# One written order for a random-feature attention and mixer kernel, with the first four quads transposed on TensorE, joined tail angles and later low-rank loads

## The chip, the cores and the metric

The kernel runs on one core of a Trainium2 chip. The metric is device time in microseconds (us), where lower is better. "PE" is TensorE, "DVE" VectorE, "ACT" ScalarE, "POOL" GpSimd and "SP" SyncE.

Ratios are the mean time of one kernel's fast runs over the mean of the other's fast runs in the same rounds, so they are not quite the ratio of the medians that are quoted beside them. Intervals in brackets are 95% intervals of the ratio.

## The reference

Attention with random features, per batch and head, and then a mixer and a two-layer network on the attention's output:

```python
batch, n_heads, seq, head_dim, n_features = 8, 8, 576, 64, 128
def phi(x):
    proj = np.einsum('bhsd,md->bhsm', x, omega)
    return np.concatenate([np.cos(proj), np.sin(proj)], axis=-1) / np.sqrt(m)
q_p, k_p = phi(q), phi(k)
kv = np.einsum('bhsm,bhsd->bhmd', k_p, v);  z = np.sum(k_p, axis=2)
num = np.einsum('bhsm,bhmd->bhsd', q_p, kv);  den = np.einsum('bhsm,bhm->bhs', q_p, z)
attn = num / den                       # den kept away from zero
x = attn.transpose(0, 2, 1, 3).reshape(8, 576, 512)
u = x + (x.transpose(0, 2, 1) @ U @ V).transpose(0, 2, 1)      # U 576x32, V 32x576
out = u + np.maximum(u @ w_ch1, 0.0) @ w_ch2                   # 512 -> 2048 -> 512
```

The network needs 1152 matmuls of 128x128 by 512 columns (576 for each layer). They are most of the work.

## The kernel before

A *group* is two heads of one batch, so there are four groups in a batch and 32 in all. A *quad* is two groups: its keys and queries are loaded by one DMA each, cast to bf16 on the way, transposed so that the head dimension lies on the partitions, and multiplied by `WT` (omega) to give angles. ACT takes their sines, POOL adds a quarter turn, ACT takes the sines again (the cosines). Then come `kv`, `num`, a normalisation `x`, the low-rank mixer (`hu`, `hn`, `hnt`) giving `u`, a DMA transpose of `u`, and the two layers `w1` and `w2`.

Every piece is an operation with a name. A planner decides the order and the PSUM banks from costs:

```python
add(("ak", g), PE, 0.27, ak, needs=kmain + ["WT"], takes=A, rank=(0, g, 0), slack=slack)
...
def order(self):                      # greedy list scheduler
    ...
            at = max([free[o.engine]] + [done[n] + o.slack for n in o.needs ...])
            ...                       # candidate banks: the one that is free first
            key = (at, o.rank)        # earliest start, then rank: attention before MLP on PE
    ...
order = plan.order()
with tc.manual_schedule():
    for o in order:
        o.emit()
```

Quad 0 is transposed on PE, with evictions on DVE and ACT. All others are transposed by DMA. The tail tokens (the ninth of nine token slots) have their own angle eviction `ut` and their own normalisation:

```python
BY_PE = (0,)
def tpd(name=name, n=n):              # quads 1 to 15
    nc.sync.dma_start_transpose(transposed(name, n), held.pop((name, n)).rearrange("p i e -> p (i e)"))
def ak(g=g, n=n):                     # 64-row matmuls
    for j in range(4):
        for e in range(2):
            r, c = at(g, 2 * j + e)
            nc.tensor.matmul(pk[:, e, j * P:(j + 1) * P], kT[r, c, :], WT[r, :])
def kv(fs, g=g, n=n):                 # 64-row matmuls: 18 with a group's sines, 18 with its cosines
    ...
            nc.tensor.matmul(kv_ps[:, hh, o], ft[r, f, 0, c:c + M], vq[n % NV][r, NS * (g % 2) + s, :], ...)
def load_low_rank():                  # on the ACT queue, early
    nc.scalar.dma_start(Vf, moe_V.unsqueeze(0).to_broadcast([4, R, S]))
    ...
```

`ak`, `at`, `aq` and `kv` use 64 of the 128 rows of the PE array, `hu` uses 32 columns of it, and `hnt` 64 columns. `w1`, `w2`, `num` and `hn` use the full array.

## Time and profile before

Three runs gave a median of 406.62 us (405.06 to 406.68). The profiled span is 404.4 us.

| engine | busy us | share of the span |
|---|---|---|
| PE | 358.1 | 89% |
| ACT | 225.7 | 56% |
| DVE | 199.4 | 49% |
| POOL | 123.1 | 30% |

The first view is the page of the kernel before: first its line of engine totals, then the busy share of PE, the granted clock of PE and the busy share of the DMA engines in 40 equal slices of the span (each digit is tenths of a slice, about 10 us wide).

```profile
PE 358.1 (89%) x3416; PEld 176.3 (44%) x3462; DVE 199.4 (49%) x340; ACT 225.7 (56%) x280; POOL 123.1 (30%) x132
...
PE   3266769689679999999999999999999999999995
PEclk9998769879959999999999999999999999999999
DMA  8999999999999787799744141023115121111223
```

PE is short of work in the first twelve slices, and the DMA engines are full in just those. The windows view of the kernel before puts numbers to it. Its columns are: stretch, length, busy time (and count) of PE, weight loads, DVE, ACT and POOL, then the granted clock, the DMA share and GB/s.

```profile
0.00:34.00 34.00, 15.66 (x272) 11.22 (x275) 18.05 (x38) 19.67 (x21) 20.85 (x32) 1.00 1.06 194
34.00:60.00 26.00, 17.73 (x189) 9.64 (x187) 12.33 (x25) 12.55 (x17) 13.11 (x15) 0.74 1.21 178
60.00:90.00 30.00, 24.70 (x267) 11.41 (x270) 17.62 (x29) 19.52 (x24) 13.64 (x15) 0.89 1.22 192
90.00:120.00 30.00, 23.74 (x320) 12.77 (x322) 21.41 (x37) 17.98 (x18) 16.88 (x17) 0.83 1.13 219
120.00:250.00 130.00, 127.78 (x1489) 62.77 (x1507) 91.83 (x154) 99.48 (x119) 51.68 (x49) 1.00 0.66 123
```

PE is busy 81.83 of the first 120 us (the sum of the first four rows), and 98% of the time from 120 to 250 us. The clock is below 1 in three of the four early stretches. A caution: the clock figure of the opening is not to be trusted. It reads 1.00 up to 34 us, but in the timeline sixteen `num` matmuls took 1.04 us at 25.45 and 0.68 us at 28.32. So clocks are compared only after 34 us below.

The table of PE's waits in the kernel before (engine and line, what it waited for, then us in total, times, longest) says for what PE stood:

```profile
PE ps L351 <- DMA kT<-kraw: 11.3, 2, 8.2
...
PE ps L561 <- DMA W2b<-in_moe_w_ch_dram: 2.9, 1, 2.9
PE ps L548 <- DMA uT<-u: 2.5, 1, 2.5
```

L351 is `ak`, which waits for keys transposed by DMA. L561 is `w2`, waiting for the last piece of W2 (used at 81.7 us). L548 is `w1`, waiting for the first transposed `u` (at 114.5 us). All three are DMA transfers.

This is the timeline of PE in the kernel before (start, duration, operation, count of matmuls run together; durations overlap by the depth of the pipeline):

```profile
170.56 1.03 PE L548 MATMUL ps<-uT,W1b 128*128 128x512 bf16 x4
171.51 0.40 PE L351 MATMUL ps<-WT,kT 64*128 64x128 bf16 x8
171.84 1.04 PE L561 MATMUL ps<-W2b,hid 128*128 128x512 bf16 x4
172.81 0.75 PE L394 MATMUL ps<-vq,ft 64*128 64x65 bf16 x36
173.40 0.38 PE L370 MATMUL ps<-qT,WT 64*128 64x512 bf16 x2
173.71 1.04 PE L548 MATMUL ps<-uT,W1b 128*128 128x512 bf16 x4
174.68 0.23 PE L362 MATMUL ps<-WT,kT 64*128 64x128 bf16 x1
```

The part of the array in use stands after the operation: `128*128` is all of it, `64*128` half.

The groups view of the kernel before gives the mean duration of the two layers' matmuls (line, form, count, busy us, mean ns, idle before):

```profile
L561 PE MATMUL ps<-W2b,hid 128*128 128x512 bf16 x537 | 140.1, 383 | 7.1 <-issue 3.4 <-DMA W2b<-in_moe_w_ch_dram 2.9
L548 PE MATMUL ps<-uT,W1b 128*128 128x512 bf16 x512 | 134.5, 389 | 2.8 <-DMA uT<-u 2.5
```

Of the 576 `w2` matmuls 537 are recorded; of all 3462 matmuls 46 are missing from this trace, although their weight loads are in it. The missing ones show as short waits for "issue" (3.4 us), so the idle time of PE in this trace is overstated, and its busy time understated, by at least that much.

### The profile page before, as it was taken

How to read it: one execution, taken by the hardware profiler on the slowest of the kernel's cores; microseconds unless marked ns; L12 is line 12 of the kernel's file. 1: busy time of each engine (PE TensorE's matmuls, PEld its weight loads, DVE VectorE, ACT ScalarE, POOL GpSimd, SP SyncE). 2: the span in 40 equal slices, each digit the busy share in tenths (PEclk: the TensorE clock that was granted, in tenths of full speed). 3: DMA queues.
4: the chain of work that ended last, by engine and by line, in shares of the span. 5: the costliest groups of instructions: out<-in, count | busy, mean ns of one | idle time of the engine just before them, and what ended most of it. 6: DMA issues, size and time to landing. Idle time of an engine off the chain costs nothing.

```text
span 404.4 us, 8121 instructions
## 1 busy us (share of the span) xinstructions
PE 358.1 (89%) x3416; PEld 176.3 (44%) x3462; DVE 199.4 (49%) x340; ACT 225.7 (56%) x280; POOL 123.1 (30%) x132
## 2 busy tenths in 40 slices
PE   3266769689679999999999999999999999999995
PEld 2155334344434444445444544544444444444442
DVE  4367436558847678777676368536313010101021
ACT  3757357564758889787696468737423333333300
POOL 5849065444653365365154023303000000000000
PEclk9998769879959999999999999999999999999999
DMA  8999999999999787799744141023115121111223
GB/s 221 162 189 171 176 196 225 207 155 206 251 192 138 152 123 160 159 192 140 170 118 73 41 92 28 2 54 78 28 39 105 26 48 31 38 43 27 52 54 79
DMA packets 75930, 46.90 MB, mean 116 GB/s; under 512 B 54644, under 2 KB 66804, under 8 KB 75892
## 3 DMA queue, kind: packets, MB, share of 16 engines
q1 hardware_dynamic: 62512, 32.22, 39.9%
q0 software_dynamic: 12672, 13.34, 22.4%
q10 hardware_dynamic: 708, 0.80, 0.6%
q8 instruction: 27, 0.44, 0.5%
q14 instruction: 11, 0.09, 0.1%
HBM read 37.21 MB, written 9.44 MB: 115 GB/s over the span
## 4 chain that ended last, share of the span: by engine, by line
PE 77%; DMA 11%; DVE 4%; issue 3%; POOL 2%; ACT 2%; POOLq 0%
PE ps L548 31%; PE ps L561 29%; PE ps L394 4%; PE ps L408 4%; DMA kT<-kraw 3%; DMA W2b<-in_moe_w_ch_dram 3%; PE ps L351 2%; DMA qraw<-in_q_dram 2%; PE ps L370 2%; POOL ang L384 2%; DMA uT<-u 2%; ACT ft L380 2%; DVE ang L329 1%; PE ps L512 1%; PE ps L413 1%
## 5 line engine op out<-in xcount | busy, mean ns | idle before, releaser
L380 ACT ACTIVATE ft<-ang 128x1024 bf16<-128x1024 int16 (+2 forms) x130 | 144.0, 1142 | 40.1 <-POOL ang L384 24.6
L553 ACT ACTIVATE hid<-ps 128x512 bf16<-128x512 f32 x144 | 85.5, 595 | 112.5 <-PE ps L548 111.9
L561 PE MATMUL ps<-W2b,hid 128*128 128x512 bf16 x537 | 140.1, 383 | 7.1 <-issue 3.4
L548 PE MATMUL ps<-uT,W1b 128*128 128x512 bf16 x512 | 134.5, 389 | 2.8 <-DMA uT<-u 2.5
L329 DVE TENSOR_SCALAR ang<-ps 128x1024 int32<-128x1024 f32 (+2 forms) x97 | 89.4, 943 | 43.3 <-PE ps L351 13.3
L384 POOL TENSOR_SCALAR ang<-ang 128x1280 int32<-128x1280 int32 (+1 forms) x64 | 73.6, 1153 | 97.3 <-ACT ft L380 96.8
L548 PEld LDWEIGHTS <-W1b 128*128 128x128 bf16 x576 | 53.2, 99 | 65.7 <-issue 8.5
L561 PEld LDWEIGHTS <-hid 128*128 128x128 bf16 x576 | 52.4, 98 | 65.2 <-issue 7.7
L573 DVE TENSOR_TENSOR o<-ps,u 128x512 f32<-128x512 f32 x32 | 22.1, 690 | 94.7 <-PE ps L561 91.4
L394 PEld LDWEIGHTS <-ft 64*128 64x128 bf16 x1152 | 23.4, 99 | 18.8 <-issue 12.1
L394 PE MATMUL ps<-vq,ft 64*128 64x65 bf16 x1152 | 28.8, 198 | 1.9 <-ACT ft L380 0.9
L408 PE MATMUL ps<-kvb,ft 128*128 128x65 bf16 x512 | 23.2, 198 | 6.1 <-ACT ft L380 5.1
L408 PEld LDWEIGHTS <-ft 128*128 128x128 bf16 x512 | 20.6, 101 | 13.0 <-ACT ft L380 5.7
L351 PE MATMUL ps<-WT,kT 64*128 64x128 bf16 x256 | 14.4, 240 | 11.9 <-DMA kT<-kraw 11.3
L287 POOL CAST vq<-vraw 128x1152 bf16<-128x1152 f32 x16 | 18.4, 1149 | 20.9 <-PE ps L394 15.8
L514 DVE TENSOR_TENSOR u<-ps,x 128x1024 bf16<-128x1024 f32 x16 | 19.5, 1221 | 6.8 <-PE ps L512 5.5
L425 DVE TENSOR_TENSOR x<-ps,rec 128x512 bf16<-128x512 f32 x32 | 22.1, 692 | 1.1
L280 POOL DMA_DIRECT2D kraw<-in_k_dram x15 | 10.9, 727 | 35.3 <-DMA kT<-kraw 35.2
L398 DVE CAST kvb<-ps 128x260 bf16<-128x260 f32 x32 | 13.6, 424 | 12.2 <-PE ps L394 12.0
L351 PEld LDWEIGHTS <-kT 64*128 64x128 bf16 x256 | 8.4, 103 | 22.4 <-DMA kT<-kraw 12.0
L548 PE MATMUL ps<-utailT,W1b 128*128 128x512 bf16 x64 | 16.4, 379 | 0.1
L370 PE MATMUL ps<-qT,WT 64*128 64x512 bf16 x64 | 13.5, 413 | 2.2 <-DVE ang L329 1.2
(60 smaller groups left out, 140.1 us busy)
## 6 DMA issues: line engine op xcount, KB each, us to landing
vraw<-in_v_dram SPq DMA_DIRECT2D x16, 576.0 KB, 4.8
out_dram<-o SPq DMA_DIRECT2D x72, 128.0 KB, 2.4
kraw<-in_k_dram POOLq DMA_DIRECT2D x15, 288.0 KB, 6.7
qraw<-in_q_dram POOLq DMA_DIRECT2D x15, 288.0 KB, 7.7
W1b<-in_moe_w_ch_dram POOLq DMA_DIRECT2D x4, 512.0 KB, 10.2
W2b<-in_moe_w_ch_dram POOLq DMA_DIRECT2D x4, 512.0 KB, 13.2
ang<-in_k_dram SPq DMA_DIRECT2D x1, 288.0 KB, 3.0
ang<-in_q_dram ACTq DMA_DIRECT2D x1, 288.0 KB, 4.7
```

The source lines that it names most:

```text
L329: nc.vector.tensor_scalar(out=dst, in0=src, scalar1=TO_UNITS, scalar2=None, op0=ALU.mult)
L351: nc.tensor.matmul(pk[:, e, j * P:(j + 1) * P], kT[r, c, :], WT[r, :])
L370: nc.tensor.matmul(pq[:, e, :], WT[r, :], held["qT", n][r, c:c + 4, :])
L380: nc.scalar.activation(out=held["ft", g].rearrange("p f a c -> p f (a c)")[:, f, lo:hi], in_=low[:, lo:hi, 0], func=ACT.Sin, scale=TO_RAD)
L384: nc.gpsimd.tensor_scalar(out=ang, in0=ang, scalar1=TURN / 4.0, scalar2=1.0, op0=ALU.add, op1=ALU.mult)
L394: nc.tensor.matmul(kv_ps[:, hh, o], ft[r, f, 0, c:c + M], vq[n % NV][r, NS * (g % 2) + s, :], start=(s == 0), stop=(s == NS - 1))
L408: nc.tensor.matmul(nd[:, t // 2, 2 * (t % 2) + hh, :], ft[:, f, 1, c:c + P], kvb[:, hh, f, :], start=(f == 0), stop=(f == 1))
L425: nc.vector.tensor_tensor(out=x[:, :, hp * P:(hp + 1) * P].rearrange("p (a t) (h d) -> p a t h d", a=2, h=2), in0=nd[:, :, 0:4, 0:D], in1= ...
L548: nc.tensor.matmul(one(("w1", b, f)), W1b[:, f // 4, ct, f % 4 * P:(f % 4 + 1) * P], uT[:, :, ct, :], start=(ct == 0), stop=(ct == NCT - 1))
L553: nc.scalar.activation(out=held["hid", b][:, f, :], in_=one(("w1", b, f)), func=ACT.Relu)
L561: nc.tensor.matmul(one(("w2", b, t, 0)), held["hid", b][:, f, t * P:(t + 1) * P], W2b[:, f, :], start=(f == 0), stop=(f == NFT - 1))
L573: nc.vector.tensor_tensor(out=o, in0=one(("w2", b, t, 0)), in1=u[:, t, :], op=ALU.add)
```

## The change

The intent is to take DMA work out of the opening, where DMA is full, to have the keys of the first quads earlier, to spare DVE some instructions, and to replace the planner by one order that was written (found elsewhere) for all engines and PSUM banks. The operations lose their costs and ranks, and a list of words `name@bank` is walked:

```diff
+ORDER = """
+begin first/k om ident first/q ld/k/0 ld/q/0 ld/k/1 ld/q/1 cast/k ldv/0 omb tpp/k/0/0@0 omt@5 tp/k/0/0 cast/q gate WT low tpp/k/0/1@6
+tpp/q/0/0@3 tp/k/0/1 tpp/q/0/1@0 tp/q/0/0 ld/k/2 ak/0@6 tp/q/0/1 uk/0 ld/q/2 ak/1@2 at/0@0 W1/0 uk/1 aq/0@5 sk/0 pk/0 uq/0 aq/1@1 sk/1
 ... (63 lines cut)
+"""
-    def order(self):                  (greedy planner, cut)
+    def run(self, order):
+        for word in order.split():
+            text, _, at = word.partition("@")
+            name = names[text]
+            _, emit, needs, takes, frees = self.ops[name]
+            assert name not in issued and all(n in issued for n in needs), word
+            if takes:
+                self.banks[name] = range(int(at), int(at) + takes)
+            ...
+            emit()
-    BY_PE = (0,)
+    BY_PE, BY_SCA = (0, 1, 2, 3), (0,)         # quads 1 to 3: nine transposes into two banks,
+                                                # one 1152-column copy on DVE
-        nc.scalar.dma_start(Vf, moe_V.unsqueeze(0).to_broadcast([4, R, S]))
+        nc.sync.dma_start(Vf, moe_V.unsqueeze(0).to_broadcast([4, R, S]))
+    add("gate", DVE, lambda: nc.vector.memset(low_f[:, S - 1:S + 1], 0.0))
+    add("low", SP, load_low_rank, needs=["gate"])
-            (nc.sync).dma_start(held["v", n], quad(v, n))          (shortened)
+            (nc.sync if n else nc.gpsimd).dma_start(held["v", n], quad(v, n))
@@ uk @@
-                units(held["ang", g][:, 0, 0:1024], ...)           (and ut: a second instruction for 256 columns)
+            for lo, hi in ((0, 512), (512, 1024)) if g == 0 else ((0, 1280),):
+                units(ang[:, lo:hi], src[:, lo:hi])
@@ norm @@
-                held["x", b] = xp.tile([P, NT, C], BF16, name="x")
+                held["x", b] = xp.tile([P, NT + 1, C], BF16, name="x")
-            nc.vector.tensor_tensor(out=x[:, :, ...], ...)         (and a second one for xtail)
+            nc.vector.tensor_tensor(
+                out=x[:, :, hp * P:(hp + 1) * P].rearrange("p t (h d) -> p h t d", h=2),
+                in0=nd[:, :, :, 0:D], in1=rec.unsqueeze(3).to_broadcast([P, 2, NT + 1, D]), op=ALU.mult)
```

Smaller parts that came along: the first keys are loaded from the ACT queue, omega is loaded without its copy, the first queries are cast on ACT, the sine's warm-up moved to the end, and the PSUM layout of `num` changed for the joined normalisation.

## The prediction

> **What bounds the kernel now.** TensorE (PE) is busy 358 of 404 us (engine table), unevenly: by the windows view 98 to 99% from 120 us on, but 82 of the first 120 us, partly at a low granted clock (0.66 in 50 to 60, 0.51 in 110 to 120). Counting matmuls at warm spacing (512 columns 0.215 us: eight take 1.90, four 1.04), I estimate only 59 us of full-clock work in the first 114.5 us: some 56 us lost there, about 20 in the rest.
>
> The DMA engines are the reason: their share is 0.9 to 1.3 in every 10 us up to 120 us, mostly below 1 later. PE's early waits are for DMA: quad 1's transposed keys at 21.8 (8.2 us), a later quad's at 51.7 (3.2), the last W2 piece at 81.7 (2.9), the first transposed u at 114.5 (2.5). The first MLP matmul starts at 41.4. The trace's DMA packets show why: one transposed 288 KB tile is 1152 packets of 256 B at 28 ns, about 2.0 us of all sixteen engines, as much as loading it (256 packets at 128 ns). A quad costs some 6 us to load and 4 more to transpose.
>
> **What the change does.**
> - Quads 1 to 3 are transposed on PE: 54 more 128-column matmuls, estimated 3 us plus pipeline ends, and six 1152-column copies on VectorE (about 0.9 us each, scaled from 0.48 for 640). This takes 12 us of DMA work out of the saturated stage, and the two longest PE waits.
> - Low-rank loads go behind the first quads; the first value load goes behind four key/query loads.
> - Tail angles join the key angles: 31 evictions of 0.41 us go, their columns add about 0.27 each to the larger one; the 0.27 us tail normalisation joins the 0.69 us one. VectorE falls some 10 us, but is half idle: little gain.
> - The written order places loads, banks and engine order anew. A second activation-table load (1.28 us) appears at the start, mostly hidden.
> - Other PE work stays: the floor after the ramp does not move.
>
> **On the critical path.** ScalarE needs about 4.6 us of sines per group (2 x 1.27 + 2 x 1.05). With keys in time, four groups take about 19 us from about 9 us: first MLP matmul estimated at 32 us, not 41.4. W2's last piece should land near 66, not 81.7 (estimated DMA work ahead of it: eight weight pieces at 3.3, five quads loaded, one transposed, 61 us). The first transposed u is used near 95, not 114.5, at equal attention progress. I expect 20 us from the ramp and a few from higher clock. The Trainium skill (TensorE: Matmul & The Clock Gate, "What's actually happening") says an idle window of about 3.4 us halves the clock; this trace agrees roughly: after the 2.88 us wait four matmuls took 1.87 us, elsewhere 1.04.
>
> **Prediction: 384 us, 373 to 396.** Faster by over 2%: 0.91; within: 0.06; slower: 0.03.
>
> **To check.** DMA share near 1 until about 95 us; no PE wait over 3 us for keys of quads 1 to 3; first MLP matmul at 30 to 35 us; PE above 97% busy from about 95 us; VectorE below 192 us; some 6900 fewer 256 B packets.
>
> **What would make it wrong.** A fixed order makes PE wait where a load is later than planned: weights or quad 4's transposes in 40 to 90 us. If weights remain the limit, the gain shrinks to about 10 us. Transposes inside the dense stage would cost a few us.

## The result and the profile after

The changed kernel took 368.5 us in the median of four runs (364.91 to 371.55, one of them slow), beside 406.65 us of the kernel before (405.06 to 407.5). The ratio is 0.9036 [0.8954, 0.9119], faster. The direction was right. The size was not: 368.5 us lies below the range of 373 to 396. A second measurement on another chip, in the last rounds, gave 367.35 us and 0.8998 [0.8956, 0.904]. All outputs are right.

The page of the kernel after, the same lines (its span is 363.1 us, so a slice is 9.1 us):

```profile
PE 346.7 (95%) x3516; PEld 178.8 (49%) x3516; DVE 195.0 (54%) x283; ACT 226.1 (62%) x282; POOL 122.2 (34%) x131
...
PE   4679999999999999999999999999999999999994
PEclk9668999999999999999999999999999999999999
DMA  8999979999989999799955920106100640052033
```

Two things happened, not one. PE's idle time fell from 404.4 - 358.1 = 46.3 us to 363.1 - 346.7 = 16.4 us. And PE's *busy* time fell by 11.4 us, although 54 matmuls were added (3462 weight loads before, 3516 after). That second fall is the one that the prediction ruled out. (The profile after has all its matmul records. With the 3.4 us of missing records moved from idle to busy, the fall in busy time is about 15 us and that in idle time about 26.5.) The windows of the kernel after:

```profile
0.00:34.00 34.00, 22.51 (x376) 17.45 (x377) 25.22 (x47) 24.90 (x26) 27.99 (x39) 0.80 1.03 207
34.00:60.00 26.00, 25.88 (x337) 14.36 (x334) 18.00 (x23) 23.21 (x30) 12.64 (x14) 1.00 1.08 175
60.00:90.00 30.00, 30.00 (x423) 16.02 (x416) 26.43 (x39) 24.03 (x26) 15.25 (x16) 1.00 1.04 179
90.00:120.00 30.00, 30.00 (x412) 15.62 (x409) 24.85 (x37) 27.36 (x32) 19.49 (x21) 1.00 0.93 198
```

PE is busy 108.39 of the first 120 us, at full clock from 34 us on. The DMA share is still about 1 up to 90 us: the engines stay as full, but with other transfers. PE's waits in the kernel after:

```profile
PE ps L310 <- DVE kraw L282: 4.4, 1, 4.4
PE ps L402 <- DVE ang L339: 2.3, 2, 1.4
PE ps L378 <- DVE ang L339: 2.3, 2, 1.4
```

The waits for transposed keys, for W2 and for `u` are gone. The 4.4 us is the start, before the first load has landed (the kernel before waits 4.2 us at the same place for omega). The timeline of PE in the kernel after, in its dense part, shows how the half-array work is bundled:

```profile
198.06 1.89 PE L554 MATMUL ps<-uT,W1b 128*128 128x512 bf16 x8
199.88 0.46 PE L402 MATMUL ps<-vq,ft 64*128 64x65 bf16 x18
200.18 0.38 PE L378 MATMUL ps<-qT,WT 64*128 64x512 bf16 x2
200.40 0.39 PE L362 MATMUL ps<-WT,kT 64*128 64x128 bf16 x8
200.62 0.22 PE L354 MATMUL ps<-WT,kT 64*128 64x128 bf16 x1
...
201.11 2.76 PE L566 MATMUL ps<-W2b,hid 128*128 128x512 bf16 x12
```

Here `kv` (L402), query angles (L378), key angles (L362) and tail angles (L354) stand next to each other, and twelve `w2` matmuls follow. I counted the round trips from full-array to part-array work and back, from the weight loads between 34 and 330 us: 106 before, 55 after. The groups of the two layers in the kernel after:

```profile
L566 PE MATMUL ps<-W2b,hid 128*128 128x512 bf16 x576 | 136.0, 379 | 0.0
L554 PE MATMUL ps<-uT,W1b 128*128 128x512 bf16 x512 | 121.8, 379 | 0.3 <-ACT hid L559 0.2
```

The means are 379 ns where they were 383 and 389: among the recorded matmuls of the two layers, 25 ran at half clock before (634 ns) and none after.

| event | before | predicted | after |
|---|---|---|---|
| first `w1` matmul, us | 41.4 | 32 | 35.5 |
| last piece of W2 landed, us | 81.4 | 66 | 57.6 |
| first `w1` on a transposed `u`, us | 114.5 | 95 | 78.5 |
| PE idle before 120 us (windows) | 38.2 | - | 11.6 |
| PE idle after 120 us (rest of the span) | 8.1 | - | 4.8 |

### The profile page after: what moved, and what is told of

It is laid out like the page before. It is cut to its first block, busy times and chain, and to the rows that moved or that the text cites. A ratio compares the mean times of both kernels' runs of the same rounds, so it can differ in the third digit from the quotient of the medians.

```text
span 363.1 us, 8210 instructions
## 1 busy us (share of the span) xinstructions
PE 346.7 (95%) x3516; PEld 178.8 (49%) x3516; DVE 195.0 (54%) x283; ACT 226.1 (62%) x282; POOL 122.2 (34%) x131
## 4 chain that ended last, share of the span: by engine, by line
PE 91%; DVE 5%; DMA 1%; POOL 1%; issue 1%; ACT 0%; POOLq 0%; DVEq 0%
PE ps L566 35%; PE ps L554 34%; PE ps L402 6%; PE ps L416 5%; DVE ang L339 3%; PE ps L362 2%; PE ps L378 2%; PE ps L519 2%; PE ps L310 1%; DMA kraw<-in_k_dram 1%; PE ps L421 1%; PE ps L527 1%; PE ps L471 1%; PE ps L473 1%; DVE x L432 1%
## 5 line engine op out<-in xcount | busy, mean ns | idle before, releaser
L559 ACT ACTIVATE hid<-ps 128x512 bf16<-128x512 f32 x144 | 84.3, 594 | 88.4 <-PE ps L554 87.7
L566 PE MATMUL ps<-W2b,hid 128*128 128x512 bf16 x576 | 136.0, 379 | 0.0
L554 PE MATMUL ps<-uT,W1b 128*128 128x512 bf16 x512 | 121.8, 379 | 0.3 <-ACT hid L559 0.2
L339 DVE TENSOR_SCALAR ang<-ps 128x1280 int32<-128x1280 f32 (+3 forms) x66 | 85.4, 1315 | 16.1 <-PE ps L378 7.2
L402 PE MATMUL ps<-vq,ft 64*128 64x65 bf16 x1152 | 25.6, 195 | 2.3 <-DVE ang L339 2.3
L402 PEld LDWEIGHTS <-ft 64*128 64x128 bf16 x1152 | 22.8, 97 | 9.1 <-issue 6.3
L432 DVE TENSOR_TENSOR x<-ps,rec 128x640 bf16<-128x640 f32 x32 | 26.4, 825 | 1.1
L416 PE MATMUL ps<-kvb,ft 128*128 128x65 bf16 x512 | 22.1, 197 | 0.8 <-DVE kvb L406 0.8
L378 PE MATMUL ps<-qT,WT 64*128 64x512 bf16 x64 | 13.8, 397 | 2.3 <-DVE ang L339 2.3
L511 DVE CAST hu<-ps 128x512 bf16<-128x512 f32 x7 | 4.8, 690 | 20.1 <-PE ps L473 14.1
L554 PE MATMUL ps<-utailT,W1b 128*128 128x512 bf16 x64 | 14.8, 379 | 0.0
L430 DVE RECIPROCAL ps<-ps 128x10 f32<-128x10 f32 x32 | 7.2, 225 | 12.3 <-PE ps L421 12.1
L362 PE MATMUL ps<-WT,kT 64*128 64x128 bf16 x256 | 13.5, 231 | 0.1
```

Source lines behind the costliest of these rows:

```text
L339: nc.vector.tensor_scalar(out=dst, in0=src, scalar1=TO_UNITS, scalar2=None, op0=ALU.mult)
L378: nc.tensor.matmul(pq[:, e, :], WT[r, :], held["qT", n][r, c:c + 4, :])
L416: nc.tensor.matmul(nd[:, hh, t, :], ft[:, f, 1, c:c + P], kvb[:, hh, f, :], start=(f == 0), stop=(f == 1))
L432: nc.vector.tensor_tensor(out=x[:, :, hp * P:(hp + 1) * P].rearrange("p t (h d) -> p h t d", h=2), in0=nd[:, :, :, 0:D], in1=rec.unsqueeze ...
L554: nc.tensor.matmul(one(("w1", b, f)), W1b[:, f // 4, ct, f % 4 * P:(f % 4 + 1) * P], uT[:, :, ct, :], start=(ct == 0), stop=(ct == NCT - 1))
L559: nc.scalar.activation(out=held["hid", b][:, f, :], in_=one(("w1", b, f)), func=ACT.Relu)
```

## The experiments

The theories at the start were these. The transposes on PE give the gain, because they free DMA in the opening; or the written order gives it, whatever does the transposes. Rivals for parts of it are the joined instructions on DVE and the held-back low-rank loads. Later the question became *why* an order makes PE's busy time shorter. Eighteen kernels were run, in five sittings, each beside the kernel before on the same chip. All are edits of the changed kernel; one is that kernel itself again.

### 1. Undo one part at a time

**Transposes of quads 1 to 3 by DMA again**, order and all else kept:

```diff
-    BY_PE, BY_SCA = (0, 1, 2, 3), (0,)
+    BY_PE, BY_SCA = (0,), (0,)
 # and the words tpp/k/1 tpp/q/1 ... tpp/k/3 tpp/q/3 taken out of ORDER
```

> The changed kernel with quads 1 to 3 transposed by DMA again, everything else and the rest of the written order kept. Theory 'transposes' (most of the 38 us comes from taking 12 us of transposes and their waits out of the DMA-bound opening): 380 to 392 us, TensorE waits of several us for quad 1 to 3 keys return, first MLP matmul after 40 us. Rival 'order' (the written order does it, wherever the transposes run): at most 374 us.

Measured: 383.89 us, 0.9405 [0.9346, 0.9464]. PE busy 346.2 us, idle 387.1 - 346.2 = 40.9 us. One line of its waits table holds the difference, the wait of the key angles for the DMA transposes:

```profile
PE ps L362 <- DMA kT<-kraw: 20.2, 2, 14.7
```

The last piece of W2 landed at 81.2 us, as before the change. But PE waits neither for W2 nor for `u` in this run: those two waits of the kernel before are gone with the written order, even where DMA still transposes. So the PE transposes are worth about 4 points of the ratio (0.9405 against 0.9036 and 0.8998, some 15 to 17 us), and it is idle time: PE's busy time is the same. (This profile is of the slowest of the five runs, 5 us above their median.) But 0.9405 alone already is a gain of 6%, with no transpose taken from the DMA engines.

**Tail joins undone**:

```diff
-            for lo, hi in ((0, 512), (512, 1024)) if g == 0 else ((0, 1280),):
+            for lo, hi in ((0, 512), (512, 1024)) if g == 0 else ((0, 1024), (1024, 1280)):
 # and norm in two instructions: x[:, 0:NT, ...] and x[r, NT, ...]
```

> The changed kernel with the VectorE joins undone: tail angles evicted by an instruction of their own, tail normalisation by its own; TensorE's order and banks kept. Theory 'transposes' and rival 'order' both: within 3 us of the changed kernel (about 371 at most), VectorE busy some 10 us more. Rival 'joins' (VectorE's latency is what lets TensorE stay dense after 120 us): 5 us or more slower, with TensorE idle gaps released by VectorE after 40 us.

Measured: 364.7 us, 0.8926 [0.8878, 0.8975]. It is not slower than the changed kernel, and might be faster; this is taken up again in the last sitting. VectorE is busy 200.3 us, 5 more than in the changed kernel and not the 10 expected.

**Low-rank loads early**:

```diff
-begin first/k om ident first/q ... cast/q gate WT low tpp/k/0/1@6
+begin first/k om low ident first/q ... cast/q WT tpp/k/0/1@6
-    add("low", SP, load_low_rank, needs=["gate"])
+    add("low", SP, load_low_rank)
```

> The changed kernel with the low-rank loads issued at the start, not held back behind a gate. All theories: 0.5 to 3 us slower, all of it before 12 us (first transposes on TensorE later), because 0.43 MB join the first loads; the rest unchanged.

Measured: 368.19 us, 0.9013 [0.8966, 0.9061], the same as the changed kernel within the intervals. The opening is later (the first W1 weight load on PE is at 39.0 us, against 35.3), but the total does not show it.

**All three undone**, so that what remains is the written order and the smaller parts that came with it:

> DMA transposes, split VectorE work and early low-rank loads all undone at once; only the written order is left of the change. Theory 'transposes': 385 to 400 us, little better than the kernel before. Rival 'order': below 380 us, at least two thirds of the gain left.

Measured: 386.49 us against 408.53, 0.946 [0.9408, 0.9511]. The time lies in the range for the theory of the transposes (385 to 400 us), but not as "little better than the kernel before"; neither theory had it right. This is the key run: 22 us of the gain of about 38 to 41 needs none of the transposes, joins and hold-back. Its page line of engine totals, and the first window:

```profile
PE 345.5 (90%) x3462; PEld 175.2 (46%) x3462; DVE 196.6 (51%) x339; ACT 226.2 (59%) x282; POOL 122.3 (32%) x131
...
0.00:34.00 34.00, 11.28 (x133) 7.27 (x134) 13.83 (x27) 17.99 (x19) 19.25 (x30) 1.00 1.12 190
```

Its number of weight loads, 3462, is that of the kernel before: the same PE work. Yet PE is busy 345.5 us, not 358.1. And its opening is *worse* than that of the kernel before (11.28 against 15.66 us busy up to 34 us). So the order's gain does not come from the first 34 us.

| kernel | span | PE busy | PE idle |
|---|---|---|---|
| before | 404.4 | 358.1 | 46.3 |
| written order, rest undone | 383.6 | 345.5 | 38.1 |
| + joins and hold-back, no PE transposes | 387.1 | 346.2 | 40.9 |
| changed kernel | 363.1 | 346.7 | 16.4 |

In these profiles the order took 12.6 us of busy time and 8.2 us of idle time; the PE transposes took 22 to 25 us of idle time and left the busy time within about 1 us. Two reservations. The first row is the only one with missing matmul records; moving at least 3.4 us from its idle to its busy time makes the order's part at least 16.0 us of busy and at most 4.8 us of idle time. (The changed kernel's second profile shows 342.3 us of busy time for the 346.7 of the first, but it lacks 35 of 3516 matmul records; complete profiles in the written order with four quads on PE show 344.9 to 347.0.) And each span is of one run: by the fast runs the transposes are worth 15 to 17 us, not the 20 to 24 of these spans.

### 2. Which part of the order?

**Other banks**: the same words, with the bank numbers dealt anew, always to the banks free for longest.

```diff
-... tpp/k/0/0@0 omt@5 ...
+... tpp/k/0/0@2 omt@0 ...        (and so on through the whole list)
```

> The changed kernel's word order unchanged, only the bank numbers dealt anew by 'the bank longest free'. If the written bank numbers matter (rival 'banks'): 4 us or more slower. Theory 'transposes plus order': within 2 us of the changed kernel.

Measured: 370.3 us, 0.9077 [0.9024, 0.9131]. At 0.4 to 0.9% above the two measurements of the changed kernel, with overlapping intervals, the choice of banks is worth nothing that can be told. The gain is in the order itself.

**The old order on the new operations**: the planner's order is mapped on the new operations, with PE transposes standing where the planner had the DMA transposes, and banks dealt as above. Then it is crossed with the written order, cut at the first `w1` matmul.

```diff
-begin first/k om ident first/q ld/k/0 ld/q/0 ld/k/1 ld/q/1 cast/k ldv/0 omb ...
+begin first/k om ident first/q ldv/0 ld/k/0 warm ld/q/0 ld/k/1 omb ...     (planner's order to the end)
```

> The changed kernel's operations (TensorE transposes, joins, gated low-rank loads) in the order that the planner of the kernel before gives, transposes placed where the planner had the DMA ones, banks dealt anew. If order and transposes each give about half (the runs with DMA transposes under the written order gave 384 to 386): 385 to 392 us. If the written order is needed for the transposes to pay: 395 or more. If the order is worth little once the transposes are on TensorE: 375 or less.

> The changed kernel's operations; its written order up to the first MLP matmul, the old planner's order after it. If the opening is what the order buys: 368 to 373 us. If the interleaving after it does (few and short TensorE waits until 120 us): 378 to 388 us, TensorE idle again between 40 and 120 us.

> The mirror of the run before: the old planner's order up to the first MLP matmul, the written order after it. First MLP matmul at 38 us or later (it is at 35.5 with the written opening, 41.4 in the kernel before). If the opening is what the order buys: 380 to 390 us; if the rest: 371 to 376.

Measured, as ratios to the kernel before (median us in brackets; the last is the run with other banks, whose banks were dealt in the same way). The old order lies where I had put it if the written order is needed for the transposes to pay (395 us or more). The other two contradict each other: the written opening with the old rest lies above both of its ranges, the old opening with the written rest in the range for a gain from the opening:

| | old rest | written rest |
|---|---|---|
| old opening | 0.9896 (402.91) | 0.947 (386.05) |
| written opening | 0.98 (400.05) | 0.9077 (370.3) |

The written rest is worth 4.3 points behind the old opening and 7.2 behind the written one. The written opening is worth 1.0 points before the old rest and 3.9 before the written one. So most lies in the rest, and an early start is kept only by a rest that can use it. With the written opening and the old rest, PE then waited 5.3 us at one time for the last piece of W2.

The run with the old order has the PE transposes and is only 1% faster than the kernel before. Its window from 20 to 30 us shows room that is not used (columns as above; the last three are clock, DMA share, GB/s):

```profile
20.00:30.00 10.00, 7.69 (x122) 6.15 (x121) 6.45 (x11) 8.51 (x8) 8.78 (x11) 1.00 0.15 36
```

The DMA engines stand at a share of 0.15, where the kernel before has 1.09: the transposes have left, and the old order issues nothing in their place. That freed DMA time is worth less because no load is issued into it fits this, but no run tests it alone.

**The old order with DMA transposes**, to see the transposes alone in the old order:

> The old planner's order with DMA transposes for quads 1 to 3, only joins and the gated low-rank loads kept of the change, banks dealt anew as in the other order runs. It checks that the rebuilt old order stands for the kernel before: 402 to 410 us, against 402.9 with the transposes on TensorE in that order. Outside 400 to 412 the order runs do not stand for the old order.

Measured: 415.41 us, 1.0146 [1.0075, 1.0218], outside what I had written down. The mapped old order is not the true old one, so runs with it are to be compared with each other only. Against the run with PE transposes (0.9896) the transposes are worth 2.5 points here, some 10 us, where they are worth 15 to 17 us in the written order. The run has two more uses. Nearly all the smaller parts of the change are in it, and it is no faster than the kernel before, so they bring no gain in this order. And it differs from the first run of part 1 (0.9405) by order and banks alone: 7.4 points, some 30 us. Both profiles have all their matmul records: PE is busy 361.7 us in the old order and 346.2 in the written one. So the fall in busy time is not an effect of missing records.

**Only the order of issue, or only that of compute**: PE, DVE and ACT in the old order with POOL and SP in the written one, and the reverse.

```diff
+# e1: words of PE, DVE, ACT in the old sequence; POOL, SP in the written sequence (about 20 words passed each other)
+# e2: the reverse (8 words passed each other)
```

> The changed kernel's operations; TensorE, VectorE and ScalarE in the old planner's order, but GpSimd and SyncE, which issue nearly all loads, transposes and stores, in the written order. Theory 'issue order' (the old order leaves the DMA engines idle near 25 us and puts key and query loads before W2): 372 to 385 us, W2's last piece by 62 us. Rival 'interleave' (TensorE's own order is what counts): 393 to 403 us.

> The mirror: TensorE, VectorE and ScalarE in the written order, GpSimd and SyncE in the old planner's. Theory 'issue order': 390 us or more, with TensorE waiting for DMA landings of keys or weights before 120 us. Rival 'interleave': 372 to 385 us.

Measured: 449.25 us, 1.0994 [1.091, 1.1078], and 427.7 us, 1.0471 [1.0415, 1.0527]. Both are slower than either pure order, so neither theory holds. The waits of PE in the first of them:

```profile
PE ps L415 <- ACT ft L387: 28.9, 2, 16.1
PE ps L401 <- POOL vq L293: 26.5, 5, 13.7
```

PE stands for sines and for widened values: the two sequences that were put together expect different things first. Which of the two halves carries the gain cannot be read from a mixture, and stays open. The second run also warns against a simple view of busy time: PE runs the written sequence in it (53 round trips between full and part of the array, a count that is explained below, against 55 in the changed kernel), and yet is busy 361.0 us, with 37 matmuls of the two layers at half clock.

### 3. Why does the order shorten PE's busy time?

The new theory, of *switches*: going from full-array to part-array matmuls costs PE time that shows as busy, and the written order does it half as often. The rival, of the *clock*: the busy time fell only because less of it ran at half clock.

The count of round trips between 34 and 330 us speaks for the switches: 106 before; 94 to 96 in the three runs with the old rest; 58 in the one with the written rest behind the old opening; 56 in the two of the first sitting that transpose by DMA; 55 in the changed kernel. The starts of the weight loads speak for it too: the step into part-array work is 0.306 us longer than its neighbours, the step back 0.10 to 0.22 us. Steps between two full-array kinds (`w1` to `w2`, `num`, `hn`) show no extra time.

The Trainium skill states the mechanism (TensorEngine Tiling (Array Packing), "Key Properties"): "Changing tiling mode (not just tile) drains the TensorE". It gives no figure. So the cost was measured by itself, where attention is over: before each of 48 `w1` pieces (blocks 6 to 8) a small matmul of 64 columns is put in that nobody needs, on 64 rows in one kernel and on 128 rows in the control. (The result stays correct: the bank is overwritten.)

```diff
             def w1(b=b, f=f):
                 uT = utailT if b == TAIL else held["uT", b]
+                if b >= 6:      # m1: 64 rows;  m2: W1b[0:128, ...] on both sides
+                    nc.tensor.matmul(one(("w1", b, f))[:, 0:64], W1b[0:64, 0, 0, 0:P], W1b[0:64, 0, 1, 0:64], start=True, stop=True)
```

> The changed kernel with one extra 64-column matmul on 64 rows of the array ahead of each of the last 48 first-layer pieces, into the bank which the piece then overwrites (results stay right). Theory 'tile switches' (each change from full-array matmuls to matmuls on part of the array and back costs about 0.44 us on TensorE, as weight loads in the traces are spaced): 18 to 24 us slower than the changed kernel. Rival 'no such cost' (the spacing is only a modelled record): at most 4 us slower.

> The control: the same extra matmuls on all 128 rows. Both theories: 1 to 4 us slower than the changed kernel, 48 times some 0.03 to 0.07 us.

Measured: 375.81 us, 0.9206 [0.9152, 0.9261] with 64 rows, and 365.18 us, 0.8943 [0.8886, 0.9] with 128 rows. The only difference is the part of the array. It costs 375.81 - 365.18 = 10.6 us, or 0.22 us for each of the 48. That is half of the 0.44 us, and of the 18 to 24 us, that I had expected from the spacing of the weight loads: the cost is real, but the spacing overstates it. The full-array dummies cost nothing that can be seen. PE's busy times, 354.2 and 343.0 us, differ by 11.2 us, so the cost is indeed booked as busy. Timeline of PE with 64 rows:

```profile
300.78 1.24 PE L568 MATMUL ps<-W2b,hid 128*128 128x512 bf16 x5
301.96 0.20 PE L554 MATMUL ps<-W1b 64*128 64x64 bf16 x1
302.09 1.04 PE L556 MATMUL ps<-uT,W1b 128*128 128x512 bf16 x4
```

and with 128 rows:

```profile
301.72 0.19 PE L554 MATMUL ps<-W1b 128*128 128x64 bf16 x1
301.75 1.03 PE L556 MATMUL ps<-uT,W1b 128*128 128x512 bf16 x4
```

The four matmuls after the dummy begin 0.13 us after its start in the first and 0.03 us in the second. In the first the dummy is late as well: five matmuls at 0.215 us, begun at 300.78, would have made room at 301.86, and it began at 301.96. The two delays of 0.10 us are about the 0.22 us that the times gave.

**More switches, in the real work**: pairs of half-array pieces are pulled apart by a full-array piece that stood next to them; all other words stay.

```diff
-... kv/4/0@1 sk/6 kv/4/1 w1/0/9@0 ...
+... kv/4/0@1 sk/6 w1/0/9@0 kv/4/1 ...
```

> The changed kernel's written order with 22 more entries into part-of-array work (82 for 60), each made by moving one such piece behind the next first- or second-layer piece; bank numbers kept. Theory 'tile switches': 8 to 11 us slower than the changed kernel. Rival 'waits only' (the order's worth lies in avoiding waits): within 3 us.

Measured: 372.82 us, 0.9129 [0.9075, 0.9184], with 76 round trips. The changed kernel on the same chip has 0.8998 and 55. That is 1.31% of 408 us, 5.3 us for 21 round trips: 0.25 us each, which agrees with the dummies, though the two intervals leave some 3 us of doubt either way, and the changed kernel's figure is of another sitting. (Against the full-row control of its own sitting, 0.8943, it would be 7.6 us, 0.36 each.) It is less than the 8 to 11 us expected at 0.44 us each, and more than waits explain: against the changed kernel's second profile PE is busy 6.3 us longer (348.6 and 342.3) and idle about 1 us longer.

**Fewer switches**: half-array pieces are moved together further.

```diff
-... ak/9@2 tp/q/5 w2/0/1/1 pq/8 uk/9 ...
+... tp/q/5 w2/0/1/1 pq/8 ak/9@2 uk/9 ...
```

> The opposite: 46 entries instead of 60, each won by moving a run of part-of-array pieces behind at most 1.8 us of full-array work, to join the next run; bank numbers kept but one. Theory 'tile switches': 4 to 6 us faster than the changed kernel (361 to 364). Rival 'waits only': no faster, or slower where a piece comes late.

Measured: 378.49 us, 0.9269 [0.9226, 0.9312], with 41 round trips. It is slower by 11 us, the wrong way for a simple reading of the switch theory. Its PE waits after 34 us say what happened:

```profile
PE ps L401 <- DVE ang L338: 4.6, 4, 1.7
PE ps L361 <- DVE ang L338: 3.5, 3, 1.4
PE ps L526 <- DVE ang L338: 2.4, 1, 2.4
...
PE ps L377 <- DVE ang L338: 0.5, 1, 0.5
```

The 14 switches saved are worth 3 us by the figures above. But PE waits 4.6 + 3.5 + 2.4 + 0.5 = 11.0 us for DVE's evictions of angles, where the changed kernel has no such wait after 34 us. The matmuls that wait (`kv`, `ak`, `hnt`, `aq`) do not read those angles. By the bank numbers in the list, each of the nine takes a PSUM bank that an angle block held just before and DVE was still emptying. The moved pieces came closer together and, but for one, kept their banks. So this run shows what bundling costs with the old banks; whether it pays with banks dealt anew was not run.

So the switch theory holds as a cost: 50 or 51 fewer round trips at 0.22 us are an estimated 11 us, half of the order's 22. The clock theory holds beside it. Of the recorded matmuls of the two layers 25 ran at half clock before, 8 with the order alone and 12 with joins and hold-back added, none after. All PE work counts here, not these alone: after 34 us the kernel before had PE busy for 20.4 us under the half clock and the order alone for 4.9, so that an estimated 10.2 and 2.5 us were lost, a difference of 7.8. Together that is an estimated 18.8 us, to set against at least 16.0 us of busy time (with the missing records put back) and 20.8 us of span. At most 4.8 us is left as less idle time, and it has not been traced to single words of the order. The sum is an account that fits, not a proof: the clock's part was not tested by a run of its own, and the second of the crossed issue and compute orders shows that PE's busy time can rise by 14 us at the same number of switches.

### 4. Can something beat both?

The changed kernel and the one with the joins undone were measured again on one chip, together with one that transposes only three quads on PE and quad 3 by DMA, issued early:

```diff
-    BY_PE, BY_SCA = (0, 1, 2, 3), (0,)
+    BY_PE, BY_SCA = (0, 1, 2), (0,)
-lowc ldv/2 uk/4 ...
+lowc tp/k/3 tp/q/3 ldv/2 uk/4 ...
```

> The changed kernel itself, so that it stands beside the next two on one chip: 363 to 370 us. The control with full-row dummies, 365.2 us, should be at most a few us above it.

> The changed kernel with the VectorE joins undone, again. If the joins are worth nothing: within 2 us of the changed kernel on the same chip, either way. If they hurt (the larger eviction holds the sine up longer): 2 to 4 us faster.

> The changed kernel with quad 3 transposed by DMA, issued ahead of the third value load, and quads 0 to 2 still on TensorE. It saves TensorE some 2 us in its dense stage and adds 4 us of DMA work ahead of W2's last piece. If DMA is no longer the limit after the opening: 1 to 3 us faster. If W2 or the loads behind it become late again: 3 us slower or more, TensorE idle between 45 and 80 us.

Measured: changed kernel 367.35 us, 0.8998 [0.8956, 0.904]; joins undone 365.84 us, 0.8975 [0.8943, 0.9007]; three quads 368.09 us, 0.9039 [0.8997, 0.9081], neither of the two outcomes for it. Each interval overlaps the others. The hint from the first sitting that the joins do harm did not hold up, nor do they help. Nothing that was run beats the changed kernel beyond the noise.

## Why the prediction was wrong

**Right for the keys: what bounded the opening, and that the transposes relieve it.** DMA was full up to 120 us, and PE waited for keys, W2 and `u`. With the transposes on PE the key waits vanish, and putting the transposes back brings 20.2 us of them back. The waits for W2 and `u` are another matter: in the written order they are absent with DMA transposes too, though W2 then lands at 81.2 us, and in the old order PE still waits 4.0 us for `u` with the transposes on PE. The order removed these two, not the freed DMA time. The estimate of 3 us for the added PE work can be neither confirmed nor refuted: PE's busy time is within about 1 us, and complete profiles differ by 2. The number of 256-byte DMA packets fell by 7,040, from 51,200 to 44,160; 6,912 of these are the six transposed tiles (some 6,900 were predicted), the rest belongs to omega. PE is full from about 40 us.

**Right in kind, too small: the half clock.** The Trainium skill (TensorE: Matmul & The Clock Gate, "What's actually happening") gives windows of 3413 ns and a clock that is either full or half. After 34 us the records of the kernel before show half clock from 37.8 to 44.6, 51.5 to 58.3, 78.8 to 85.6 and 109.5 to 119.7 us: two, two, two and three such windows long. The changed kernel has none after 29.2 us. The prediction had a few us for this; half of the 20.4 us that PE was busy in these stretches is an estimated 10 us. Its example does not show what it was given for: the clock had fallen at 78.8 us, when the 2.9 us wait for W2 only began. In the 3.4 us before that PE was busy for 1.7.

**Not shown: that the second table load is mostly hidden.** ACT in the opening of the kernel after (start, duration):

```profile
6.93 1.23 ACT L314 COPY qT<-ps 128x512 bf16<-128x512 bf16 x2 [1.72 <-PE ps L310]
8.17 1.28 ACT L388 ACT_TABLE_LOAD   x1
9.46 2.53 ACT L388 ACTIVATE ft<-ang 128x512 bf16<-128x512 int16 x3
```

The first sine starts right behind the load, at 9.46 us, against 8.36 before. So at this place the load is not hidden. What it costs in the end was not tested.

**Wrong, the step that failed: "Other PE work stays: the floor after the ramp does not move."** PE's busy time was taken as a floor. It fell by 11.4 us. With the written order alone, at an unchanged number of matmuls, it fell by 12.6 us, and by at least 16.0 us with the missing records of the profile before. The runs put in its place a cost per change between full and part of the array: 0.22 us (dummies) and 0.25 us (pieces pulled apart), and a count that went from 106 to 55 (after 120 us, where the prediction saw no gain, from 74 to 30). The trace of before had shown it: 4 us of timeline with three such changes. The prediction said that the written order "places loads, banks and engine order anew" and gave it no term of its own. It was worth 22 us, more than half of the result, of which the switches are an estimated 11 us and the half clock an estimated 8.

**Wrong in size, and by size the larger miss: "I expect 20 us from the ramp."** Counted as the prediction counted (time elapsed minus the work done so far at full speed, an estimate from matmul spacings), the kernel before had lost 58.7 us by 120 us and the changed one 22.9. The ramp gave 36 us, not 20. The rest of the span gave 8.4 us, and the added transposes took an estimated 3 back: 36 + 8 - 3 = 41, the difference of the two profiled spans. The predicted milestones were too late: W2's last piece came at 57.6 us and not 66, the first transposed `u` at 78.5 and not 95. Only the first `w1` was later than predicted, 35.5 against 32 us. The prediction treated the DMA queue as a fixed list with 12 us taken out. But what the room is worth depends on the order: some 10 us in the old one, 15 to 17 in the written one.

**Wrong, without effect: "VectorE below 192 us".** It is 195.0 us, 4.4 us less than before and not 10. The six copies of 1152 columns (0.75 us each, 4.5 us together) had been listed, but not added to the sum. As predicted, DVE's busy time was not what counted: the joins are worth nothing that can be measured.

**Not settled.** Which words of the order save the rest of the idle time (at most 4.8 us), how much of the half clock is the order's doing in every run, and whether the sequence of issue or of compute carries more of the gain.

## What to carry to other kernels

A busy engine is not yet a floor: before pricing its busy time as fixed, look in the timeline for changes of array part and for half-clock matmuls, count them, and give them a cost. Before trusting a split into busy and idle, compare the counts of matmuls and weight loads: missing records look like idle time. Part-array matmuls are best bundled, but a bundle needs PSUM banks that are already empty: the run with the fewest switches, with its bank numbers kept, waited 11 us for banks and was 11 us slower. Taking work off full DMA engines was worth more in an order that was made for it, so a change of place and a change of order should be predicted, and tested, together.

## What the Trainium skill lacked or had wrong

- TensorEngine Tiling (Array Packing), "Key Properties": it says that a change of tiling mode drains TensorE. The runs show a cost that fits this, but the page gives no figure. Here a round trip from the full array to 64 rows and back cost 0.22 us (48 dummies, 10.6 us) and 0.25 us (21 in the real work). It shows in the profile as busy time, not as a wait. Steps between kinds of full-array matmuls showed no extra time (weight loads 0.216 us apart, as within a kind).
- ScalarE: Activation LUTs, "What ACT_TABLE_LOAD costs": it gives about 1283 ns for the load and some 1380 ns of drain for a switch. The load took 1.28 us here, but no drain of that size shows: the copy before it ended at 8.16 us, the load began at 8.17, and the sine behind it at 9.46.
- DMA: Bandwidth & Descriptors, "Latency and other measured facts": it gives 261 GB/s for a DMA transpose with a non-contiguous middle dimension. One 294,912-byte tile was 1152 packets, in the kernel before of 28 ns in the mean and 18 in the median. Over 16 engines that is an estimated 146 GB/s by the mean and 228 by the median, while other loads ran beside it. So it does not show the page wrong; a figure under load is what is lacking.
- TensorE: Matmul & The Clock Gate, "What's actually happening": it has the half clock come after an idle window. Here it came after windows that were not empty: in the 3.4 us before the four falls of the kernel before (37.8, 51.5, 78.8 and 109.5 us) PE was busy for 2.1, 0.4, 1.7 and 1.8 us. How idle a window must be was not measured. The clock of the opening could not be checked, because the records read 1.00 where the same sixteen matmuls took 1.04 us at one time and 0.68 us at another.
